# A short convolution before a maxout layer: the first GpSimd block later, ten such blocks for twelve, and a new early order

## The chip, the cores and the metric

The kernel runs on one core of a Trainium2 chip. The time is the device time of one execution in microseconds (us). Five runs of the kernel before gave a median of 463.79 us, from 463.38 to 464.07.

A core has TensorE (PE: matmuls, with weight loads listed apart as PEld), VectorE (DVE), ScalarE (ACT), GpSimd (POOL) and SyncE (SP, which here only issues DMAs). Each runs its own instructions in the order of the program and waits for the others by semaphores.

## The reference

x has 8 sequences of 4160 rows of 192 channels. First each channel is convolved along its sequence with seven taps: the taps of a head (24 channels share one) are the softmax of a row of `weight`, and rows ahead of the sequence are zero. The result, taken as 33280 rows y, goes through a maxout layer with 768 hidden values and back to 192 channels:

```python
out = np.einsum('hk,bskhg->bshg', softmax(weight), x_unf)   # x_unf: seven rows, shifted
h = np.maximum(np.maximum(y @ w1, y @ w2), y @ w3)
return h @ w_out
```

The kernel uses max(a, b, c) = max(a - c, b - c, 0) + c: `wd` holds w1 - w3 and w2 - w3, so that one Relu and one maximum give h - y w3, and the product y (w3 w_out), whose 192 x 192 matrix `m16` is made once, is added in the second layer.

## The kernel before

**Blocks.** The rows are cut into 65 blocks of 512 (`NB`), done one after the other by the loop over `t` at the end; blocks 0 and 1 are done ahead of it, together with the preparation of the weights. The convolution of a block is done in one of three ways.

- Blocks 0 to 3 (`conv_dense`, `cross`) use banded matmuls on fp16 copies of x, which give y with channels on partitions directly.
- Most blocks are *row blocks*. `load_x` (line 123) brings x as 70 rows (six of them for the overlap) times eight pieces; `cast_x` (L165, GpSimd, two instructions) makes it fp16; `conv` (L387) does a pair of blocks in 16 matmuls with a band matrix that has 70 rows and two column halves, a *burst*; `evac` (L438, two copies on ScalarE and two on VectorE) writes it to `ys`; `turn` (L447) transposes it by a DMA, so that channels come to partitions; and `double` (L457) copies the two halves of the partitions crosswise by two DMAs, so that both halves of the array have their operand. The tiles are named `yd`.
- Some are *GpSimd blocks*, whose indices are in `qpos` (L71): 11, 16, ... 61 and 64, twelve in all. `load_q` brings x (tile `xl`), `cast_q` makes it fp16, `turn_q` transposes it by a DMA (`xt<-xq`), `lead_q` copies the six rows ahead of it (`xt<-xt`), and `tap_q` (L221) does one tap at a time on GpSimd: three multiplications by a tap's weights (L229), one addition (L237, and L240 for the last). Then `double` follows as for the others.

**The layers.** `l1(t, j)` (L490) does a sixth of the hidden values: six matmuls of 64 rows and 512 columns. Two work at a time, one on the upper 64 rows of the array into `lp`, one on the lower 64 into `lq`; ScalarE takes the Relu of `lp` into `r` (L503), and VectorE the maximum of `r` and `lq` into `h` (L504). `lp` has two PSUM buffers (pool `psp`) and `lq` two (`psq`), and a burst takes one of each and two of `psw`. `st2(t, u, 6)` (L508) does a sixth of the second layer of the block before: matmuls of 64 rows and 192 columns, again on the upper and the lower half in turn (`i` = 0 and 1), five of each; ScalarE and VectorE add the halves (L560, L561) into `outs`, which `store` writes.

**One block of the loop** (L659 on). SP and GpSimd get their work first: the load of block t + 6, the crosswise copies for t + 2, the transposes and casts that are due, then the row block t + 5 is cast. Then comes `l1(t, 0)`, and, in two blocks of five, a burst (`convs_at`), three blocks ahead of the first of its pair. Just before the burst one matmul of the second layer is put, on the upper rows alone (`st2` with `first_half_only`, L536, a *filler*). Behind the burst come the evacuations, `turn(t + 3)`, the store of block t - 2, and the taps that `plan` gives to this block; then `st2(t - 1, 0)` and, in turn, the rest of both layers.

**The early blocks** have their own order. `plan` (L645 to L657) gives the first GpSimd block, 11, seven taps in blocks 5 to 8, and the last, 64, half a block for each tap; all between have their seven taps spread over five blocks, the first tap seven blocks ahead of the block itself. In block 2 SP loads blocks 7 and 8 and the first `xl`; in block 3 it issues the copies for block 4, the second `xl`, the transposes of blocks 5 and 6, the load of block 9, and `spread_w(0)` (L321, the seven weights of each channel written to DRAM as `wide`); in block 4 the copies for blocks 5 and 6. The store of block 0 is issued by GpSimd (L639), which has a queue of its own. In the preparation `make_wd(2, 4)` (L610) stands on VectorE behind `l1(0, 1)`.

Of the kernel before, what the change touches and what calls it, by code (L numbers as in the profile page):

```python
# [10 lines left out]
FP16 = mybir.dt.float16  # L11
# [3 lines left out]
P = 128  # L15
KW = 7
# [11 lines left out]
def kernel(  # L28
# [39 lines left out]
        blocks.append(segs)  # L68
    NB = len(blocks)
    EVERY = 5  # L70
    qpos = [q for q in range(11, NB - 3, EVERY)] + [NB - 1]  # L71
    qset = set(qpos)
    ENDS = NB - 7
    ends = blocks.pop()
# [33 lines left out]
    accp = ctx.enter_context(tc.tile_pool(name="accp", bufs=2))  # L108
    x16p = ctx.enter_context(tc.tile_pool(name="x16p", bufs=3))
    ysp = ctx.enter_context(tc.tile_pool(name="ysp", bufs=3))  # L110
    ydp = ctx.enter_context(tc.tile_pool(name="ydp", bufs=6))
    rp = ctx.enter_context(tc.tile_pool(name="rp", bufs=4))
    hp = ctx.enter_context(tc.tile_pool(name="hp", bufs=2))
    tp = ctx.enter_context(tc.tile_pool(name="tp", bufs=2))
# [332 lines left out]
    def turn(t):  # L447


        if t >= NB or t in qset:  # L450
            return
        t0, u, nu = place(t)
        yd = dense[t] = ydp.tile([P, 2, NCH // 2, P], FP16, tag="yd", name=f"yd_{t}")
        nc.sync.dma_start_transpose(out=yd[:, 0, :, :],
                                    in_=slots[t0][:, u, :, :].rearrange("p r d -> p (r d)"))

# [51 lines left out]
    def st2(t, u, NU, first_half_only=False):  # L508
# [24 lines left out]
        todo, ps = halves[t]  # L533
        n = len(todo[0])
        es = range(n * u // NU, n * (u + 1) // NU)
        for e in es[:1] if first_half_only else es:  # L536
            for i in range(2):
                if first_half_only:
                    if i:
                        break  # L540
                    ahead.add((t, e))
                elif i == 0 and (t, e) in ahead:
                    continue
                s, first, last, (a, b) = todo[i][e]
                b0 = s if t == NB - 1 else s - s % 2
                if (b0, i) not in ps:
                    pool, tag = (psw, "w")
                    if t == NB - 1 and s in (1, 2):
                        pool, tag = (psp, "p") if i == 0 else (psq, "q")
                    ps[b0, i] = pool.tile([P, 2, D], FP32, tag=tag, name=f"po{i}_{t}_{s}")  # L550
                nc.tensor.matmul(ps[b0, i][:, s % 2, :], lhsT=a, rhs=b, start=first, stop=last)  # L551
            ends = {todo[i][e][0] for i in range(2) if todo[i][e][2]}
            for s in sorted(ends):
                done[t, s] = done.get((t, s), 0) + sum(todo[i][e][0] == s and todo[i][e][2] for i in range(2))
                if done[t, s] < 2 or (s % 2 == 0 and t < NB - 1):
                    continue
                s0 = s if t == NB - 1 else s - 1
                ss = slice(s0 % 2, s % 2 + 1)
                a = tp.tile([P, 2, D], FP32, tag="a", name=f"a_{t}_{s}")
                nc.scalar.copy(out=a[:, ss, :], in_=ps[s0, 0][:, ss, :])  # L560
                nc.vector.tensor_add(out=outs[t][:, s0:s + 1, :], in0=a[:, ss, :],  # L561
                                     in1=ps[s0, 1][:, ss, :])
                if t == NB - 1 and s == 1:
                    store(t, 0, 2, (nc.sync,))
                elif t == NB - 1 and s == 3:
                    store(t, 2, 3, (nc.scalar,))
                    store(t, 3, 4, (nc.sync,))
# [37 lines left out]
    cast_w3(0)  # L605
    conv_dense(1, (nc.scalar.copy, nc.scalar.copy, nc.scalar.copy))
    cross(1)
    l1(0, 1)
    keep_warm(2)
    make_wd(2, 4)  # L610
    l1(1, 0)
    cast_w3(1)
    l1(1, 1, WW)
# [22 lines left out]
    l1(1, 5)  # L636
    for u in range(1, NJ):
        st2(0, u, NJ)
    store(0, 0, 4, (nc.gpsimd,))  # L639

# [2 lines left out]
    doubles_at = {2: (), 3: (4,), 4: (5, 6)}  # L645
    plan = {}
    for n, q in enumerate(qpos):
        w = min(4 + EVERY * n, NB - 7)
        load, cast, turned, lead = (1, 3, 4, 4) if n == 0 else (w - 6, w - 3, w - 2, w - 1)
        when = {0: (5, 5, 6, 6, 7, 7, 8), len(qpos) - 1: [w + k // 2 for k in range(KW)]}.get(  # L650
            n, [w + k * EVERY // KW for k in range(KW)])
        for what, at in (("load", load), ("cast", cast), ("turn", turned), ("lead", lead)):
            plan.setdefault(at, {})[what] = q
        for k in range(KW):
            plan.setdefault(when[k], {}).setdefault("taps", []).append((q, k))
    for t in range(2, NB):
        todo = plan.get(t, {})  # L657
        if t > 4:
            load_x(t + 6)  # L659
        for u in doubles_at.get(t, (t + 2,)):  # L660
            double(u)
        if t == 4:
            load_x(t + 6)
        if t > 3 and "turn" in todo:
            turn_q(todo["turn"])
        if t > 4 and "lead" in todo:
            lead_q(todo["lead"])
        if t > 3:
            cast_x(t + 5)
# [20 lines left out]
        if t == 2:  # L690
            turn(4)
            load_x(8)
            load_q(plan[1]["load"])
            cast_x(5)
            cast_x(6)
        elif t == 3:
            turn(5)
            turn(6)
            load_x(9)
            cast_x(7)  # L700
            cast_x(8)
        else:
            turn(t + 3)
        if t == 3:
            spread_w(0)
        if t == 4:
            spread_w(1)
            lead_q(todo["lead"])
        if 2 < t:
            store(t - 2, 0, 4, (nc.sync,))  # L710
        if "cast" in todo:
            cast_q(todo["cast"])
        for q, k in todo.get("taps", ()):
# [41 lines left out]
```

## Time and profile before

| | |
|---|---|
| five runs, median | 463.79 us |
| profiled execution: its time, its span | 463.79 us, 462.0 us |
| granted clock of TensorE | full speed in all 40 slices |
| share of the 16 DMA engines taken by SP's queue (q1) | 80.4% of the span |
| read from HBM, written to HBM | 29.85 MB, 25.56 MB |
| GpSimd: taps (L229), additions (L237, L240), casts of x (L176) | 116.1, 108.6, 21.7, 77.9 us |
| GpSimd waiting for x ahead of its casts | 59.0 us |
| VectorE: maximum (L504); ScalarE: Relu (L503) | 264.5 us; 230.5 us |

The span is what the profiler sees between the first and the last instruction; the time has 1.8 us around it. Busy times say how long an engine worked, not what the end waits for. The view that tells is the chain of work that ended last, followed back from the last instruction: each piece is there because the next one waited for it. The list of waits gives, for an engine and a line, whose work ended its idle time, with the total in us, how often, and the longest. A timeline gives start, length, engine, line and tiles of each instruction. For a DMA that SP issues, the length is that of the issue alone; the landing is a separate event in the trace (a semaphore that counts sixteen pieces).

### The profile page before, as it was taken

What the parts mean: (1) busy time and instruction counts of PE and PEld (TensorE: products, weight loads), DVE (VectorE), ACT (ScalarE), POOL (GpSimd) and SP (SyncE); (2) the same over time, 40 slices, a digit from 0 to 9 for tenths busy, and PEclk for the clock granted to TensorE, in tenths of its full rate; (3) what the DMA queues carried; (4) which work ended last, traced back from release to release, by engine and by line L of the source; (5) the groups of instructions that cost most, each with busy time, mean ns of one, the idle gap of its engine ahead of it and who ended that gap; (6) DMA issues with size and microseconds to landing.
All of it is one profiled execution on the core that took longest, in us unless ns stands there. A gap on an engine that the chain in (4) does not pass through costs nothing.

```text
span 462.0 us, 17259 instructions
## 1 busy us (share of the span) xinstructions
PE 454.4 (98%) x6969; PEld 369.2 (80%) x6969; DVE 354.2 (77%) x595; ACT 314.3 (68%) x597; POOL 352.5 (76%) x501
## 2 busy tenths in 40 slices
PE   8999899999999999999999999999999999999997
PEld 4577688977877887888888888888888888888886
DVE  6877677778787777777878777777878777777775
ACT  5767576667676666767676676766767676676664
POOL 5753399999977988978977968967968969969500
PEclk9999999999999999999999999999999999999999
DMA  8969999899878988788688697698598797874423
GB/s 189 222 147 211 168 188 184 197 206 225 187 127 200 191 164 214 176 179 188 164 184 189 159 217 174 148 208 201 134 210 177 167 222 176 159 176 92 100 70 104
DMA packets 137527, 80.77 MB, mean 175 GB/s; under 512 B 58294, under 2 KB 137368, under 8 KB 137448
## 3 DMA queue, kind: packets, MB, share of 16 engines
q1 hardware_dynamic: 137176, 79.18, 80.4%
q8 instruction: 54, 0.88, 0.9%
q0 software_dynamic: 112, 0.39, 0.3%
q14 instruction: 25, 0.20, 0.1%
q10 hardware_dynamic: 160, 0.10, 0.1%
HBM read 29.85 MB, written 25.56 MB: 120 GB/s over the span
## 4 chain that ended last, share of the span: by engine, by line
PE 90%; POOL 5%; DMA 3%; issue 1%; DVE 0%; ACT 0%; SPq 0%; POOLq 0%; DVEq 0%
PE lq L499 35%; PE po L551 33%; PE lp L499 14%; PE G L397 4%; POOL tap L237 2%; POOL tap L229 2%; DMA xf<-in_x_dram 2%; PE idle L294 1%; DMA xt<-xq 1%; PE D L415 1%; DMA xt<-xt 1%; POOL x L176 1%; PE lw L499 0%; PE band_cols L335 0%; DVE wd L352 0%
## 5 line engine op out<-in xcount | busy, mean ns | idle before, releaser
L504 DVE TENSOR_TENSOR h<-r,lq 128x512 f16<-128x512 f16 x386 | 264.5, 685 | 99.4 <-ACT r L503 99.1
L503 ACT ACTIVATE r<-lp 128x512 f16<-128x512 f32 x386 | 230.5, 597 | 134.5 <-PE lp L499 123.6
L499 PE MATMUL lp<-yd,wd 64*128 64x512 f16 x1158 | 312.3, 376 | 1.9 <-DMA yd<-yd 1.4
L499 PE MATMUL lq<-yd,wd 64*128 64x512 f16 x1158 | 312.1, 376 | 0.4 <-DVE yd L431 0.4
L551 PE MATMUL po<-wo,h 64*128 64x192 f16 x3120 | 263.2, 243 | 0.0
L551 PEld LDWEIGHTS <-h 64*128 64x128 f16 x3120 | 209.0, 94 | 21.1 <-issue 0.3
L499 PEld LDWEIGHTS <-wd 64*128 64x128 f16 x2340 | 161.9, 94 | 38.6 <-DMA yd<-yd 2.0
L176 POOL CAST x<-xf 70x768 f16<-70x768 f32 x98 | 77.9, 823 | 59.1 <-DMA xf<-in_x_dram 59.0
L229 POOL TENSOR_SCALAR tap<-xt,wcol 128x256 f32<-128x256 f16 x252 | 116.1, 478 | 5.7 <-DMA xt<-xt 5.3
L237 POOL TENSOR_TENSOR tap<-tap,tap 128x768 f32<-128x768 f32 x60 | 108.6, 1810 | 5.0
L551 PE MATMUL po<-m,yd 64*128 64x192 f16 x780 | 109.0, 243 | 0.0
L561 DVE TENSOR_TENSOR o<-a,po 128x384 f32<-128x384 f32 (+1 forms) x132 | 71.4, 541 | 0.6 <-ACT a L560 0.6
L551 PEld LDWEIGHTS <-yd 64*128 64x128 f16 x780 | 61.7, 94 | 11.7
L560 ACT COPY a<-po 128x384 f32<-128x384 f32 (+1 forms) x132 | 62.2, 472 | 2.3 <-PE po L551 2.3
L443 DVE CAST ys<-G 128x384 f16<-128x384 f32 x49 | 24.9, 549 | 0.7 <-PE G L397 0.6
L397 PEld LDWEIGHTS <-band 70*64 70x64 f16 x400 | 15.8, 110 | 10.0 <-PE lp L499 9.1
L240 POOL TENSOR_TENSOR yd<-tap,tap 128x768 f16<-128x768 f32 x12 | 21.7, 1812 | 1.0
L397 PE MATMUL G<-x,band 70*64 70x192 f16 (+1 forms) x400 | 21.2, 248 | 0.8 <-POOL x L176 0.8
L443 ACT CAST ys<-G 128x384 f16<-128x384 f32 x49 | 21.1, 483 | 0.9 <-DMA yd<-yd 0.9
L198 POOL CAST xq<-xl 128x384 f16<-128x384 f32 x24 | 11.4, 505 | 0.0
L256 POOL CAST xz<-xf 112x80 f16<-112x80 f32 (+2 forms) x18 | 5.2, 330 | 4.5 <-DMA xf<-in_x_dram 3.5
L294 PE MATMUL idle<-idle 128*128 128x512 f16 x15 | 6.6, 590 | 1.2 <-DVE idle L289 1.2
(52 smaller groups left out, 68.5 us busy)
## 6 DMA issues: line engine op xcount, KB each, us to landing
out_dram<-o SPq DMA_DIRECT2D x61, 384.0 KB
xf<-in_x_dram SPq DMA_DIRECT2D x47, 420.0 KB
yd<-yd SPq DMA_DIRECT2D x122, 96.0 KB
xl<-in_x_dram SPq DMA_DIRECT2D x12, 384.0 KB
xf<-in_x_dram SPq DMA_DIRECT2D x5, 367.5 KB
ws<-in_moe_w_dram SPq DMA_DIRECT2D x6, 192.0 KB
out_dram<-o SPq DMA_DIRECT2D x5, 192.0 KB
yd<-ys SPq DMA_TRANSPOSE x49
```

The costliest lines, as they stand in the source:

```text
L176: nc.gpsimd.tensor_copy(out=x16s[t0][0:K, :, c, u, :, :].rearrange("p h r c -> p r h c"), in_=xf[0:K, c:NR:2, :].rearrange("p r (h c) -> p ...
L229: nc.gpsimd.tensor_scalar(out=part[:, 2 * c:2 * c + 2, :], in0=xt[:, 2 * c:2 * c + 2, LEAD - PAD + k:LEAD - PAD + k + P], scalar1=wcol[:, ...
L237: nc.gpsimd.tensor_add(out=accs[q][:], in0=accs[q][:], in1=part[:])
L240: nc.gpsimd.tensor_add(out=yd[:, 0, :, :], in0=accs.pop(q)[:], in1=part[:])
L397: nc.tensor.matmul(G[h // per][HALF * c:HALF * (c + 1), h % per, :], lhsT=band[0:HALF + PAD, h, PAD:HALF + PAD], rhs=x16s[t0][0:HALF + PAD ...
L443: copy(out=slots[t][:, :, :, GRP * per * i:GRP * per * (i + 1)].rearrange("p u r (h c) -> p h (u r) c", c=GRP), in_=G[i][:].rearrange("p h ...
L499: nc.tensor.matmul(ps[i][:, 0:N], lhsT=wd[row, c, P * j:P * (j + 1)], rhs=y_all(t, i, c), start=(c == 0), stop=(c == NC - 1))
L503: nc.scalar.activation(out=r[:, 0:N], in_=ps[0][:, 0:N], func=AF.Relu)
L504: nc.vector.tensor_max(out=hs[t][:, j, 0:N], in0=r[:, 0:N], in1=ps[1][:, 0:N])
L551: nc.tensor.matmul(ps[b0, i][:, s % 2, :], lhsT=a, rhs=b, start=first, stop=last)
L560: nc.scalar.copy(out=a[:, ss, :], in_=ps[s0, 0][:, ss, :])
L561: nc.vector.tensor_add(out=outs[t][:, s0:s + 1, :], in0=a[:, ss, :], in1=ps[s0, 1][:, ss, :])
```

## The change

- GpSimd blocks are 15, 20, ... 60: ten for twelve. All have their taps by the same rule; the special cases for the first and the last are gone. So block 15's first tap is due in block 8, and blocks 11, 16, 61, 64 and so on become row blocks or change places. The row blocks are 51 in place of 49: one more pair, one more burst.
- Row blocks are loaded seven blocks ahead in place of six, and on SP the load stands behind the crosswise copies. In block 2 SP loads block 9 in place of the first `xl`, in block 3 block 10 in place of the second `xl` and block 9; the first `xl` comes in block 4.
- `spread_w(0)` and `spread_w(1)` move from blocks 3 and 4 to blocks 4 and 5, behind the copies that are issued at the head of these blocks.
- The store of block 0 goes from GpSimd's queue to SP's, in block 2, behind the loads.
- `make_wd(2, 4)` goes ahead of `l1(0, 1)` on VectorE.
- Two fillers stand ahead of each burst.
- The tiles `yd` of row blocks get a pool of their own with six buffers; the others keep four.

```diff
--- before.py
+++ after.py
@@ -68,7 +68,7 @@
         blocks.append(segs)
     NB = len(blocks)
     EVERY = 5
-    qpos = [q for q in range(11, NB - 3, EVERY)] + [NB - 1]
+    qpos = [q for q in range(15, NB - 4, EVERY)]
     qset = set(qpos)
     ENDS = NB - 7
     ends = blocks.pop()
@@ -108,7 +108,8 @@
     accp = ctx.enter_context(tc.tile_pool(name="accp", bufs=2))
     x16p = ctx.enter_context(tc.tile_pool(name="x16p", bufs=3))
     ysp = ctx.enter_context(tc.tile_pool(name="ysp", bufs=3))
-    ydp = ctx.enter_context(tc.tile_pool(name="ydp", bufs=6))
+    ydp = ctx.enter_context(tc.tile_pool(name="ydp", bufs=4))
+    ypp = ctx.enter_context(tc.tile_pool(name="ypp", bufs=6))
     rp = ctx.enter_context(tc.tile_pool(name="rp", bufs=4))
     hp = ctx.enter_context(tc.tile_pool(name="hp", bufs=2))
     tp = ctx.enter_context(tc.tile_pool(name="tp", bufs=2))
@@ -450,7 +451,7 @@
         if t >= NB or t in qset:
             return
         t0, u, nu = place(t)
-        yd = dense[t] = ydp.tile([P, 2, NCH // 2, P], FP16, tag="yd", name=f"yd_{t}")
+        yd = dense[t] = ypp.tile([P, 2, NCH // 2, P], FP16, tag="yp", name=f"yp_{t}")
         nc.sync.dma_start_transpose(out=yd[:, 0, :, :],
                                     in_=slots[t0][:, u, :, :].rearrange("p r d -> p (r d)"))
 
@@ -533,7 +534,7 @@
         todo, ps = halves[t]
         n = len(todo[0])
         es = range(n * u // NU, n * (u + 1) // NU)
-        for e in es[:1] if first_half_only else es:
+        for e in es[:2] if first_half_only else es:
             for i in range(2):
                 if first_half_only:
                     if i:
@@ -605,9 +606,9 @@
     cast_w3(0)
     conv_dense(1, (nc.scalar.copy, nc.scalar.copy, nc.scalar.copy))
     cross(1)
+    make_wd(2, 4)
     l1(0, 1)
     keep_warm(2)
-    make_wd(2, 4)
     l1(1, 0)
     cast_w3(1)
     l1(1, 1, WW)
@@ -636,7 +637,6 @@
     l1(1, 5)
     for u in range(1, NJ):
         st2(0, u, NJ)
-    store(0, 0, 4, (nc.gpsimd,))
 
 
 
@@ -645,25 +645,24 @@
     doubles_at = {2: (), 3: (4,), 4: (5, 6)}
     plan = {}
     for n, q in enumerate(qpos):
-        w = min(4 + EVERY * n, NB - 7)
-        load, cast, turned, lead = (1, 3, 4, 4) if n == 0 else (w - 6, w - 3, w - 2, w - 1)
-        when = {0: (5, 5, 6, 6, 7, 7, 8), len(qpos) - 1: [w + k // 2 for k in range(KW)]}.get(
-            n, [w + k * EVERY // KW for k in range(KW)])
+        w = q - 7
+        load, cast, turned, lead = max(4, w - 6), w - 3, w - 2, w - 1
         for what, at in (("load", load), ("cast", cast), ("turn", turned), ("lead", lead)):
-            plan.setdefault(at, {})[what] = q
+            assert what not in plan.setdefault(at, {})
+            plan[at][what] = q
         for k in range(KW):
-            plan.setdefault(when[k], {}).setdefault("taps", []).append((q, k))
+            at = w + k * EVERY // KW
+            assert at < q - 2
+            plan.setdefault(at, {}).setdefault("taps", []).append((q, k))
     for t in range(2, NB):
         todo = plan.get(t, {})
-        if t > 4:
-            load_x(t + 6)
         for u in doubles_at.get(t, (t + 2,)):
             double(u)
-        if t == 4:
-            load_x(t + 6)
-        if t > 3 and "turn" in todo:
+        if t > 3:
+            load_x(t + 7)
+        if "turn" in todo:
             turn_q(todo["turn"])
-        if t > 4 and "lead" in todo:
+        if "lead" in todo:
             lead_q(todo["lead"])
         if t > 3:
             cast_x(t + 5)
@@ -690,24 +689,22 @@
         if t == 2:
             turn(4)
             load_x(8)
-            load_q(plan[1]["load"])
+            load_x(9)
             cast_x(5)
             cast_x(6)
         elif t == 3:
             turn(5)
             turn(6)
-            load_x(9)
+            load_x(10)
             cast_x(7)
             cast_x(8)
         else:
             turn(t + 3)
-        if t == 3:
+        if t == 4:
             spread_w(0)
-        if t == 4:
+        if t == 5:
             spread_w(1)
-            lead_q(todo["lead"])
-        if 2 < t:
-            store(t - 2, 0, 4, (nc.sync,))
+        store(t - 2, 0, 4, (nc.sync,))
         if "cast" in todo:
             cast_q(todo["cast"])
         for q, k in todo.get("taps", ()):
```

## The prediction

> **What bounds the kernel now.** I read the page's busy times first, then the waits of TensorE, then the chain that ended last, then the timelines of SP and TensorE around the places that the chain names. From the page, parts 1 and 4:
>
> ```profile
> PE 454.4 (98%) x6969; PEld 369.2 (80%) x6969; DVE 354.2 (77%) x595; ACT 314.3 (68%) x597; POOL 352.5 (76%) x501
> ...
> PE 90%; POOL 5%; DMA 3%; issue 1%; DVE 0%; ACT 0%; SPq 0%; POOLq 0%; DVEq 0%
> ```
>
> TensorE is the bound, but 8% of the chain is GpSimd and DMA. The waits of TensorE (total, times, longest) name the two places:
>
> ```profile
> PE lp L499 <- DMA yd<-yd: 1.4, 1, 1.4
> ...
> PE G L397 <- POOL x L176: 0.8, 2, 0.5
> ```
>
> The chain in order of time (start, length, piece) shows where they lie, and what the steady state costs:
>
> ```profile
> 42.92 7.04 DMA xf<-in_x_dram
> 50.02 5.07 DMA xt<-xq
> 55.15 3.14 DMA xt<-xt
> ...
> 78.59 1.54 POOL x L176 x2
> 80.18 0.82 PE G L397 x15
> ...
> 215.17 0.85 PE G L397 x16
> ...
> 228.85 0.85 PE G L397 x16
> ...
> 248.93 0.85 PE G L397 x16
> ```
>
> After 100 us nothing but TensorE stands on the chain. From the starts of the first-layer groups in the TensorE timeline (1.06 apart, six to a block) a block takes 6.36. Two blocks with one convolution burst take 228.85 - 215.17 = 13.68, three with one 20.08; so a burst costs 0.96 or 1.00, **0.98 on average**.
>
> Block starts in the same timeline give the early losses. Blocks 3, 4, 5 begin at 35.02, 42.53, 51.67 and block 6 at 58.13: 23.11 us, where two blocks with a burst and one without need 2 x 7.34 + 6.36 = 21.04. **2.07 lost.** Block 9 takes 8.35 instead of 7.36: **0.99 lost.** Nothing else from block 3 on is over its price.
>
> **Part 1, ten GpSimd blocks for twelve.** Two blocks go from GpSimd to TensorE, which is one more pair, one more burst (24 to 25 of the paired kind): **+0.98**. Its four evacuations (2 x 483 ns on ScalarE, 2 x 549 ns on VectorE) lie in that price, for the bursts that I measured have them too. GpSimd loses 2 x (21 x 0.478 + 6 x 1.81 + 2 x 0.505 + 0.2) = 44 us and gains four casts, 4 x 0.823 = 3.3 us. It is off the path after 100 us, so that is worth nothing there.
>
> **Part 2, the first GpSimd block at 15.** The taps of block 11 were due from block 5 (51.67) but began at 58.47, after late transfers, and are squeezed into 3.5 blocks; so the casts of blocks 12 and 13 stood behind them until 80.13, and block 9's burst waited. Now the first tap is due at block 8, spread over five blocks like all later ones, which never wait. GpSimd casts block 9 in block 4 and block 10 in block 5, ahead of their burst in block 6. **-0.99**; bounds -0.99 and 0.
>
> **Part 3, the early order on SP.** Block 4 needs the two copies that complete its operand (issued at 38.00), block 5 the next two (44.95). From SP's timeline (start, length of issue):
>
> ```profile
> 34.92 0.44 SPq L188 DMA_DIRECT2D xl<-in_x_dram  x1
> 38.00 1.14 SPq L462 DMA_DIRECT2D yd<-yd  x2
> 39.18 0.59 SPq L188 DMA_DIRECT2D xl<-in_x_dram  x1
> 39.88 2.94 SPq L454 DMA_TRANSPOSE yd<-ys  x2
> 42.92 0.52 SPq L144 DMA_DIRECT2D xf<-in_x_dram  x1
> 43.49 0.84 SPq L324 DMA_DIRECT2D wide<-line  x1
> 44.38 0.47 SPq L580 DMA_DIRECT2D out_dram<-o  x1
> 44.95 3.82 SPq L462 DMA_DIRECT2D yd<-yd  x4
> ```
>
> The trace's landing events show a queue that is served in this order: the `xl` of 34.92 lands at 41.40, the copies at 42.48 and 42.79 (block 4 starts at 42.53), the transposes at 44.35 and 44.99, the `xf` at 49.96, `wide` at 50.16, the store at 51.40, and block 5's first copy at 51.62 (block 5 starts at 51.67).
>
> *Block 5's copies.* Of the `xf` of 42.92 most pieces are in by 47.4; then DMA thins out (205 GB/s in 47-49 us, 148 in 49-51, after 250 in 45-47) and the store behind it lands 3 us later, though a store elsewhere follows its forerunner by 1.15 (214.97 to 216.13). Between them stands only `wide`, 192 pieces of 14 bytes written to DRAM. I take it as the cause. The Trainium skill (DMA: Bandwidth & Descriptors, Specifications) says that transfers under 512 B are done as read-modify-write; that would fit, and this trace shows the delay but not its mechanism. The change moves `wide` a block later, behind these copies. Then they land at 45.0 (transposes) + 2.4 (`xf`) + 1.15 (store) + 0.25 = 48.8, before block 5 can start. If `wide` is innocent they land near 51.6 as now.
>
> *Block 4's copies.* Ahead of them the queue had `xl` (512 pieces of 768 B). Now it has block 9's `xf` (560) and block 0's store (512), which leaves GpSimd's queue for SP's. Reads ran at 283 pieces per us (566 in 38-40), stores at 450 (900 in 214-216): + 48/283 + 512/450 = +1.3. Off that goes about 0.2, since the store no longer runs beside the first transfers (it landed at 32.77): landing near 42.48 + 1.1 = 43.6. Without a wait block 4 would start at 35.02 + 7.34 = 42.36. So it waits 1.3, +0.1 for the second copy (0.12 now). Bounds: most of the 16 pieces of the first copy are in by 41.1 now, one is late at 42.48; without the late one the wait is 0, and with another `xf` like the 7.04 one (5 us where 2.4 is usual) it is 3.9.
>
> So block 5 starts at 42.36 + 1.4 + 7.34 = 51.1, its copies there already: of 2.07 lost, 1.4 stays. **-0.67**; bounds -2.07 and +1.8. The stall does not go; it moves a block forward.
>
> The Trainium skill (the same page, Issuing engines are not separate DMA queues) says that DMAs of all engines share the same engines, and another queue saves only issue time. By that, moving the store costs nothing and this term would be -1.8. Here the row differs, for order counts: issued at 28.61 the store was through before the copies joined; on SP's queue it stands ahead of them.
>
> **Part 4, loads seven ahead, more buffers, loads behind the copies on SP.** SP waits up to 3.4 us (42.3 in all) at such copies for a transpose, and each load behind is now that much later, but a whole block (6.36) earlier in the program. GpSimd's waits for `xf` (59 us) go; they held nothing except in part 2. Separate pools keep SP's transposes from waiting for a buffer; TensorE doesn't wait for them after 100 us. 0.
>
> **Part 5, early VectorE order.** `make_wd(2, 4)` (0.95) goes ahead of the maximum of l1(0, 1), from 15.32 to about 14.72. TensorE's wait for it (0.57 at 16.33) would go, but l1(0, 2) also takes the PSUM buffer that this maximum frees, and that now ends at 14.72 + 0.95 + 0.69 = 16.36. The one wait takes the other's place: 0; bounds -0.57 and +0.95.
>
> **Part 6, two fillers.** A filler is a second-layer matmul on the upper 64 rows, put ahead of the burst, while the lower rows still stream:
>
> ```profile
> 214.67 0.38 PE L499 MATMUL lp<-yd,wd 64*128 64x512 f16 x1
> 214.87 0.38 PE L499 MATMUL lq<-yd,wd 64*128 64x512 f16 x1
> 214.89 0.24 PE L551 MATMUL po<-m,yd 64*128 64x192 f16 x1
> 215.17 0.85 PE L397 MATMUL G<-x,band 70*64 70x192 f16 x16
> 215.96 0.26 PE L551 MATMUL po<-m,yd 64*128 64x192 f16 x2
> ```
>
> In all 24 bursts the first band weights load 303 to 305 ns after the last `lq` starts, however long the filler has run (180 to 300 ns). So the lower rows set the burst. A second filler starts 82 ns after the first (the pitch of such matmuls), where 160 to 220 ns are free. And behind the burst the lower rows still have their five matmuls before the next `lp`, which never overtakes them. I take 0. Bounds: 82 ns off each of 25 bursts, -2.05; or 82 ns on each, +2.05.
>
> **Sum**, against the profiled execution (463.79 for a span of 462.0; the median of the five is 463.79 too): 0.98 - 0.99 - 0.67 + 0 = -0.68, so **463.1 us**. Runs within 0.2% (462.86 to 464.72) can't be told from no change here.
>
> **Rivals.**
> 1. *The early waits go altogether*: block 4's copies land in time, for the one late piece is chance. For it: 15 of its 16 pieces are in by 41.58 now. Against: the store is in the way. 0.98 - 0.99 - 2.07 = -2.08: 461.7.
> 2. *Fillers pay*: 82 ns off each burst. For it: the upper rows idle there. Against: the fixed 304 ns. 463.1 - 2.05 = 461.05.
> 3. *Slower: the second filler holds the band's weights back*, as it may if they wait for its end (243 ns) rather than its stream: at 82 ns a burst 465.15. It decides from (464.72 - 463.1)/25 = 65 ns a burst. Against: a filler 180 ns old didn't hold them.
> 4. *GpSimd is not relieved*: another burst waits as block 9's did, 464.1. Against: five blocks per seven taps never waited.
>
> **Chances.** Forecast 0.52 (462.3 to 463.9; 0.17 of it faster, 0.35 the same); rival 1 0.18; rival 2 0.08; rival 3 0.10; rival 4 0.08 (same); a new early wait of over 1.6 us 0.04. Faster 0.17 + 0.18 + 0.08 = 0.43; same 0.35 + 0.08 = 0.43; slower 0.14. The range takes in rival 1 and the small end of rival 3: 461.2 to 464.7.
>
> **What would show it.** Block 4 starting near 43.6 and block 5 near 51.1 (part 3; block 5 still near 51.7 with its copies late would clear `wide`); block 9 without GpSimd ahead of its burst; 25 bursts whose weights load 304 ns after `lq`; 6.36 per block. A burst price off 0.98, or waits of TensorE after block 6, would make it wrong.

## The result, and the profile after

The kernel after took 467.48 us (median of 53 runs, 463.18 to 475.47); the kernel before, beside it, 464.26 (95 runs, 462.59 to 469.66). The ratio is **1.0045 [1.0032, 1.0059]**: slower by about 2.1 us, where 0.7 less was forecast. Single runs of this kernel scatter far more than those before, and the ratio leaves out those over 1.5% above the fastest (13 of 53), so it is smaller than the quotient of the medians (1.0069). The forecast of 463.1 is where its quickest runs lie.

The profiled execution took 470.98 us, 3.5 more than the median, with a span of 469.1. The page's busy times and shares of the chain:

```profile
PE 455.6 (97%) x6985; PEld 357.1 (76%) x6985; DVE 354.9 (76%) x597; ACT 317.6 (68%) x599; POOL 311.2 (66%) x444
...
PE 91%; DMA 6%; DVE 1%; SPq 1%; issue 0%; POOL 0%; ACT 0%; DVEq 0%; POOLq 0%
```

GpSimd has left the chain (5% before) and has 41 us less to do, as meant. DMA has doubled its share to 6%. The list of waits, over all engines (total, times, longest):

```profile
DVE o L562 <- DMA out_dram<-o: 3.6, 2, 3.1
PE lq L500 <- DVE h L505: 3.5, 3, 2.9
...
PE lp L500 <- DMA yp<-yp: 2.2, 1, 2.2
```

The third line is the early wait for the crosswise copies, as before. The first two are new: VectorE's addition of the halves, into an output buffer, waits for a *store* out of that buffer, and TensorE then for VectorE. (Lines are one higher than before: L500 is the first layer, L505 the maximum, L562 the addition, L581 the store.) The chain in order of time shows both places:

```profile
32.93 5.76 DMA yp<-ys
38.76 6.90 DMA yp<-yp
...
114.42 0.60 ACT r L504
115.04 0.42 DVE h L505
115.46 6.42 DMA out_dram<-o
122.48 0.69 DVE h L505
...
214.10 0.81 PE G L398 x16
227.77 0.81 PE G L398 x16
```

The store issued at 115.46 lands at 121.88, and TensorE's work stands behind it. Two blocks with one burst take 227.77 - 214.10 = 13.67 at the end of the list, as they did (13.68).

The starts of the blocks (first matmul of `l1(t, 0)` in the TensorE timeline) cut the span into stretches. A second profile of the same kernel, and two of the experiments below, stand beside:

| us | before | after | after, again | loads first | loads first, more PE |
|---|---|---|---|---|---|
| to block 2 | 27.05 | 27.87 | 28.15 | 27.11 | 27.33 |
| block 2 to block 6 | 31.08 | 31.52 | 30.77 | 30.91 | 29.53 |
| block 6 to block 64 | 391.45 | 396.08 | 396.59 | 390.89 | 390.89 |
| block 64 to the last matmul | 9.15 | 9.19 | 9.19 | 9.19 | 9.19 |
| last matmul to the end | 3.28 | 4.43 | 4.10 | 4.33 | 3.40 |
| span | 462.01 | 469.10 | 468.80 | 462.43 | 460.34 |

The differences of after add up to 0.83 + 0.44 + 4.63 + 0.04 + 1.15 = 7.09. Nearly all is in the long stretch, and there in three blocks: 13 (+0.53 over its price), 14 (9.84, +3.48) and 15 (8.50, +1.19), 5.2 in all. In the second profile it is blocks 20 and 23 to 25 (+5.7): the place changes from one execution to the next. **The end is the other: 0.8 to 1.2 us more between the last matmul and the end, in both.**

Not all of the 5.2 is waiting. TensorE stands still for 0.35 us at 113.42 and for 2.90 us at 120.31, 3.25 in all. Just behind that pause its granted clock is half of full speed for 3.41 us, from 123.64 to 127.05. The first line here is the granted clock in 40 slices of the span, in tenths (9 is 90% or more); the others are bursts from the chain, of which the second falls into that stretch:

```profile
PEclk8999999999899999999999999999999999999999
...
107.76 0.81 PE G L398 x16
...
126.28 1.20 PE G L398 x16
...
146.67 0.78 PE G L398 x16
```

Block 15 waits for nothing; its 1.19 us lie in that stretch. Half of 3.41 is 1.7 us, my estimate of the cost: with the waits 4.95 of the 5.2. The second profile has the same, a pause of 2.44 us at 188.22 and half the clock from 190.60 to 194.01. The kernel before and loads first have no such stretch before their last matmul.

### The profile page after: what moved, and what is told of

Read it like the earlier page. It is cut to its first block, busy times and chain, and to the rows that moved or that the text cites. A ratio compares the mean times of both kernels' runs of the same rounds, so it can differ in the third digit from the quotient of the medians.

```text
span 469.1 us, 17240 instructions
## 1 busy us (share of the span) xinstructions
PE 455.6 (97%) x6985; PEld 357.1 (76%) x6985; DVE 354.9 (76%) x597; ACT 317.6 (68%) x599; POOL 311.2 (66%) x444
## 4 chain that ended last, share of the span: by engine, by line
PE 91%; DMA 6%; DVE 1%; SPq 1%; issue 0%; POOL 0%; ACT 0%; DVEq 0%; POOLq 0%
PE lq L500 39%; PE po L552 36%; PE lp L500 11%; PE G L398 4%; DMA xf<-in_x_dram 2%; DMA yp<-yp 1%; DMA out_dram<-o 1%; DMA yp<-ys 1%; PE D L416 1%; PE lw L500 1%; DVE h L505 1%; SPq L270 0%; POOL xz L257 0%; SPq L145 0%; PE pm L381 0%
## 5 line engine op out<-in xcount | busy, mean ns | idle before, releaser
L505 DVE TENSOR_TENSOR h<-r,lq 128x512 f16<-128x512 f16 x386 | 264.3, 685 | 99.8 <-ACT r L504 97.1
L552 PE MATMUL po<-wo,h 64*128 64x192 f16 x3120 | 273.7, 243 | 0.0
L500 PE MATMUL lq<-yp,wd 64*128 64x512 f16 x918 | 247.4, 376 | 3.3 <-DVE h L505 3.3
L500 PE MATMUL lp<-yp,wd 64*128 64x512 f16 x918 | 248.2, 377 | 2.2 <-DMA yp<-yp 2.2
L500 PEld LDWEIGHTS <-wd 64*128 64x128 f16 x2340 | 158.1, 94 | 50.7 <-issue 5.6
L230 POOL TENSOR_SCALAR tap<-xt,wcol 128x256 f32<-128x256 f16 x210 | 96.7, 477 | 55.9 <-DMA xt<-xt 55.9
L177 POOL CAST x<-xf 70x768 f16<-70x768 f32 x102 | 81.1, 822 | 29.5 <-DMA xf<-in_x_dram 22.4
L238 POOL TENSOR_TENSOR tap<-tap,tap 128x768 f32<-128x768 f32 x50 | 90.4, 1809 | 4.2
L552 PE MATMUL po<-m,yp 64*128 64x192 f16 x612 | 92.6, 244 | 0.0
L562 DVE TENSOR_TENSOR o<-a,po 128x384 f32<-128x384 f32 (+1 forms) x132 | 71.4, 541 | 4.5 <-DMA out_dram<-o 3.6
L500 PE MATMUL lp<-yd,wd 64*128 64x512 f16 x240 | 66.0, 381 | 0.5 <-DVE wd L353 0.5
L500 PE MATMUL lq<-yd,wd 64*128 64x512 f16 x240 | 65.6, 380 | 0.2 <-DVE h L505 0.2
L552 PEld LDWEIGHTS <-yp 64*128 64x128 f16 x612 | 50.7, 94 | 14.0 <-issue 0.3
L552 PE MATMUL po<-m,yd 64*128 64x192 f16 x168 | 23.8, 243 | 0.0
```

Source lines behind the costliest of these rows:

```text
L177: nc.gpsimd.tensor_copy(out=x16s[t0][0:K, :, c, u, :, :].rearrange("p h r c -> p r h c"), in_=xf[0:K, c:NR:2, :].rearrange("p r (h c) -> p ...
L230: nc.gpsimd.tensor_scalar(out=part[:, 2 * c:2 * c + 2, :], in0=xt[:, 2 * c:2 * c + 2, LEAD - PAD + k:LEAD - PAD + k + P], scalar1=wcol[:, ...
L238: nc.gpsimd.tensor_add(out=accs[q][:], in0=accs[q][:], in1=part[:])
L500: nc.tensor.matmul(ps[i][:, 0:N], lhsT=wd[row, c, P * j:P * (j + 1)], rhs=y_all(t, i, c), start=(c == 0), stop=(c == NC - 1))
L505: nc.vector.tensor_max(out=hs[t][:, j, 0:N], in0=r[:, 0:N], in1=ps[1][:, 0:N])
```

## Where the late wait comes from: the order on SP

Why is a store late at 115? SP's timeline of after (start, length of issue):

```profile
102.89 1.13 SPq L463 DMA_DIRECT2D yp<-yp  x2
104.12 0.53 SPq L145 DMA_DIRECT2D xf<-in_x_dram  x1
104.75 1.23 SPq L204 DMA_TRANSPOSE xt<-xq  x1
106.08 1.47 SPq L455 DMA_TRANSPOSE yp<-ys  x1
107.63 0.54 SPq L581 DMA_DIRECT2D out_dram<-o  x1
111.62 1.11 SPq L463 DMA_DIRECT2D yp<-yp  x2
```

The copies of 102.89 had to wait for their transpose; only then comes the load (its last piece lands at 108.73), and the transposes are queued behind it: that of 106.08 lands at 111.61. At 111.62 SP goes on, for the next copies wait for just that transpose. So copies, load and transpose form one chain, one turn of it 8.73 us here, where a block takes 6.36 or 7.32, and the stores of each block stand behind it on SP. In the kernel before, the load goes out ahead of the copies and runs while SP waits for them. The two sides in the lists of SP's waits, after:

```profile
SPq L463 <- DMA yp<-ys: 106.9, 50, 3.7
```

and the kernel after with its loads ahead of the copies again (e1_load_first):

```profile
SPq L463 <- DMA yp<-ys: 54.4, 41, 3.7
```

Before it was 42.3. The longest wait hardly differs; the sum does. From 90 to 420 us a transpose from `ys` lands (median) 3.06 us after its issue before, 4.52 in after and 3.78 with the loads first. I call *lag* the time from the start of a block to the issue of its store (that of block t - 2). Before, it is 1.6 to 5.6 us from block 12 on. In after it is 8.2 in block 4 and 13.0 in blocks 7 and 8, then 10.3, 11.9, 13.6 in blocks 9 to 11 and 15.0 in block 12. That is the store of block 10, and with its 6.42 to the landing its buffer is free 21.4 us after block 12 began. There are three output buffers, so the addition of block 13 needs it again, and VectorE was ready for that 18.5 us after block 12 began (118.91): it waits 3.1.

My theory at this point: it is the order alone, with the long stretch of row blocks (5 to 14) that the later first GpSimd block leaves. Rivals: the store of block 0 on SP (part 3), or the fillers (part 6).

**After, unchanged** (e1_after_again, beside the next three on one chip).

> The changed kernel itself, a second profile of it. Theory A (SP's loop: the load of x stands behind the crosswise copies, which wait for a transpose, so stores come late and VectorE waits for an output buffer): about 1.0045 times the kernel before, and the profile again has waits of VectorE for the landing of a store somewhere in blocks 12 to 16, of 1 to 5 us in all, besides 1.3 to 2.5 us lost in block 3. Rival B (only the early order costs): time 1.0045 as well, but nothing lost after block 5; the 5.2 us lost in blocks 13 to 15 of the first profile would be an accident of that execution.

469.08 (464.71 to 471.33), 1.0094 [1.0061, 1.0128].

**Loads first** (e1_load_first):

```diff
+        if t > 4:
+            load_x(t + 7)
         for u in doubles_at.get(t, (t + 2,)):
             double(u)
-        if t > 3:
+        if t == 4:
             load_x(t + 7)
```

> The changed kernel with the load of x back ahead of the crosswise copies on SP from block 5 on, still seven blocks ahead. Theory A: no wait in blocks 12 to 16, 2 to 4 us less than the changed kernel of the same call, so 0.995 to 1.000 of the kernel before; the loss in block 3 stays. Rival B: same time as the changed kernel, within 0.5 us. Rival C (too much DMA work in the stretch of row blocks from 5 to 14, whatever the order): waits in blocks 12 to 16 stay, gain under 1 us.

464.40 (463.50 to 466.17), 1.0002 [0.9983, 1.0022]. The scatter is gone, no wait for a store is in the profile, and the lag is at most 5.4 us from block 12 on. This one edit is worth 4.7 us between the medians: without the new order the late wait does not come. The granted clock is part of it: the clock lost, (1 - granted share) x span, averages 1.9 us over the ten runs of after and 0.4 over these twelve, so by this estimate about 1.5 of the 4.3 us between their means is clock.

**The store of block 0 on GpSimd's queue again** (e1_store0_pool):

```diff
-        store(t - 2, 0, 4, (nc.sync,))
+        store(t - 2, 0, 4, (nc.sync if t > 2 else nc.gpsimd,))
```

> The changed kernel with the store of block 0 back on GpSimd's queue, still in block 2. Theory A: the loss ahead of block 4 falls by the store's 1.1 to 1.5 us, the waits in blocks 12 to 16 stay; 0 to 1.5 us less than the changed kernel. Rival B: 2 us or more less than the changed kernel, no loss after block 5.

469.42 (464.36 to 473.50), 1.0090 [1.0060, 1.0121]: as slow as after, so this rival is out. That rests on the times: the profile is of one of the quicker runs (465.99), its lag is at most 11.0 from block 12 on, and no late wait is in it.

**One filler** (e1_one_filler):

```diff
-        for e in es[:2] if first_half_only else es:
+        for e in es[:1] if first_half_only else es:
```

> The changed kernel with one filler ahead of each burst as before. In the first profile of the changed kernel a burst cost 0.957 us each time, in the kernel before 0.96 and 1.00 in turn. If the second filler is what takes the 0.04 off every second burst, bursts cost 0.96 and 1.00 again and the time is 0.5 us longer than the changed kernel; if it does nothing, bursts stay at 0.957 and the time is the same within 0.3 us.

468.68 (464.25 to 475.51), 1.0056 [1.0024, 1.0088]: slow too, and VectorE waits 4.0 us for stores in its profile, so the second filler is not the cause either.

**The order in the kernel before** (e2_before_load_behind), and **a fourth output buffer in after** (e2_outs4):

```diff
-        if t > 4:
-            load_x(t + 6)
         for u in doubles_at.get(t, (t + 2,)):
             double(u)
-        if t == 4:
+        if t > 3:
             load_x(t + 6)
```

> The kernel before with one part of the change alone: from block 5 on the load of x stands behind the crosswise copies on SP (six blocks ahead as before). Theory A: SP's waits at the copies for a transpose rise from 42 us to 80 or more, stores come late, and it is 1 to 6 us slower than the kernel before, with a wide spread; waits of VectorE for a store's landing or of TensorE for casts appear after block 9. Rival C (the longer stretch of row blocks is what overloads the queue, the order matters only there): within 0.5 us of the kernel before.

```diff
-    outp = ctx.enter_context(tc.tile_pool(name="outp", bufs=3))
+    outp = ctx.enter_context(tc.tile_pool(name="outp", bufs=4))
```

> The changed kernel with four output buffers in place of three. If the late stores cost time through the output buffer alone, the waits of VectorE for a store's landing go, and the time falls by 2 us or more against the changed kernel (to about 1.000 to 1.004 of the kernel before); SP's waits at the copies stay near 115 us. If SP's lateness reaches TensorE by another way as well (copies or casts late), the time stays within 1 us of the changed kernel.

The first took 464.48 (463.19 to 465.83), **1.0007 [0.9984, 1.0030]**. SP waits 115.8 us at its copies, more than in after, and the lag hovers between about 5 and 10 us; but it never climbs to 15, and nothing that TensorE needs is late. So the order alone is not enough: what else of the change it takes (the long stretch, the loads seven blocks ahead or another part) this run does not say. The second took 464.66 (463.01 to 470.94), 1.0010 [0.9982, 1.0038]: SP waits as in after (101.2 us), the lag reaches 11.5, and 9 of 12 runs lie between 463.0 and 465.1. Of the 53 runs of after 10 are that quick. In most runs, then, the buffer is the way by which the late store reaches TensorE. But three runs took 469.0 to 470.9. What they wait for no profile shows; their granted clock was 0.991 to 0.994, that of the other nine 0.998 to 1.0.

**The long stretch taken away** (e4_after_q11): the first GpSimd block at 11 again, prepared in blocks 2 to 5, with ten such blocks (11 to 56) and all else as in after:

```diff
-    qpos = [q for q in range(15, NB - 4, EVERY)]
+    qpos = [q for q in range(11, NB - 8, EVERY)]
...
-        load, cast, turned, lead = max(4, w - 6), w - 3, w - 2, w - 1
+        load, cast, turned, lead = (2, 3, 4, 5) if n == 0 else (max(4, w - 6), w - 3, w - 2, w - 1)
...
-            at = w + k * EVERY // KW
+            at = (5, 5, 6, 6, 7, 7, 8)[k] if n == 0 else w + k * EVERY // KW
...
-        if t == 4:
+        if t == 3:
             spread_w(0)
-        if t == 5:
+        if t == 4:
             spread_w(1)
```

> The changed kernel, its load still behind the copies, with ten GpSimd blocks at 11, 16, ... 56 in place of 15 to 60 (the first with its taps in blocks 5 to 8 and the seven weights spread in blocks 3 and 4, as in the kernel before). If the ten row blocks in a row at the start are what drives SP late when its order is the changed one, SP's stores stay within 12 us of their place, no wait for a store's landing shows, and the time is 2 us or more below the changed kernel, 0.999 to 1.003 of the kernel before. If the order alone does it, it is as slow and as widely spread as the changed kernel (1.005 to 1.010).

471.90 (471.39 to 475.64), 1.0187 [1.0160, 1.0214]. No store is late in its profile (lag at most 10.6). But block 9 loses 5.2 us behind late taps (3.2 of it waiting for casts; the clock is at half for 3.41 us behind that), and in such a pause SP catches up: the lag falls from 10.4 to 2.6. So it does not tell whether the stretch or the pause keeps the lag down: that both the order *and* the stretch are needed is not shown. The second profile of after speaks against it in part: there the late store is waited for in block 24, where every fifth block is a GpSimd block as before, though the lag had stayed above 9 since block 5.

**Stores issued by ScalarE** (e3_stores_act). This was to take the stores out of SP's chain and leave the order as it is:

```diff
-        store(t - 2, 0, 4, (nc.sync,))
+        store(t - 2, 0, 4, (nc.scalar if 2 < t < NB - 4 else nc.sync,))
```

> The changed kernel, its load still behind the copies, with the stores of blocks 1 to 58 issued by ScalarE on its own queue, when their block's turn comes. If it is SP's order of issue alone that makes stores late, no wait of VectorE for a store's landing is left in the profile, and the time falls by 2 us or more against the changed kernel, to 0.998 to 1.002 of the kernel before, with a narrow spread; if the DMA engines themselves are behind, the stores land late on any queue and waits stay, as slow and as widely spread as the changed kernel.

550.29 (545.63 to 556.95), 1.1829 [1.1782, 1.1877], for another reason. The chain of this kernel in a window:

```profile
202.79 2.17 DMA yp<-yp
...
205.04 0.42 ACTq L581
```

ScalarE's issue comes right after the landing of copies (204.96) whose data it has no use for. In the trace both DMAs count on one semaphore, of which the kernel's DMAs share eight; 21 of the 60 DMAs that ScalarE issues behind an earlier one on the same semaphore start 0.07 to 0.08 us after its landing, and none before it. So ScalarE's Relus stand behind SP's waits: they wait 57.8 us for copies. About 28 of the 86 us over the kernel before lie in the clock, whose granted share averages 0.948 here (the estimate from above). The question that the run was meant for stays open.

## The early order, and `wide`

**Copies ahead** (e2_copies_first, on loads first): the copies for block 4 go ahead of block 9's load and block 0's store, which stood before them in SP's queue.

```diff
         for u in doubles_at.get(t, (t + 2,)):
             double(u)
+        if t == 3:
+            load_x(9)
+            store(0, 0, 4, (nc.sync,))
...
-            load_x(9)
...
-        store(t - 2, 0, 4, (nc.sync,))
+        if t > 2:
+            store(t - 2, 0, 4, (nc.sync,))
```

> The changed kernel with loads ahead of the copies, and in block 3 the copies for block 4 ahead of the load of block 9 and of the store of block 0, which follow them and so stand between these copies and the two transposes. If the loss in block 3 comes from what stands ahead of the copies on SP's queue and from the transposes directly behind them, block 3 takes 7.3 to 7.7 in place of 8.9, block 4 waits at most 0.5, and the time is 1.0 to 1.8 us less than with the loads ahead alone: 0.996 to 0.998 of the kernel before. If the loss is due to the lateness of the first transpose, it stays.

464.57 (462.15 to 467.25), 1.0008 [0.9986, 1.0030]. Block 4 now starts with no wait (42.84, block 3 + 7.31), where 1.55 were lost in loads first. Block 5 then waits 1.83, and the stretch from block 2 to 6 takes 30.90 against 30.91. In this pair the order says only which block pays; that the early transfers as a whole are the limit is my reading of it.

**Both, and the end mended** (e3_copies_first_more_pe: the same, with block 1's store behind the copies for 5 and 6, and the extra instructions of the next section):

```diff
         if t == 4:
+            store(1, 0, 4, (nc.sync,))
             load_x(t + 7)
...
-        if t > 2:
+        if t > 3:
             store(t - 2, 0, 4, (nc.sync,))
```

> Loads ahead of the copies, the early 76 TensorE instructions, the copies for block 4 ahead of the load of block 9 and the store of block 0, and the store of block 1 behind the copies for blocks 5 and 6. With the copies for block 4 first, block 5 waited 1.8 us for its own; with one store less ahead of them it should wait 0.5 to 1.0. Then blocks 3 to 5 lose 0.5 to 1.0 in all, and the time is 0.994 to 0.998 of the kernel before. If the transposes and not the queue set these landings, block 5 loses 1.8 again: 0.998 to 0.999.

464.12 (461.55 to 465.48), 0.9989 [0.9968, 1.0010]: blocks 4 and 5 wait 0.1 together, but block 2 takes 1.05 and block 6 0.5 over their price. No gain.

**Block 0's store on GpSimd's queue, block 10's load ahead of the transposes, more PE** (e3_store0_cushion_more_pe, on loads first):

```diff
         elif t == 3:
+            load_x(10)
             turn(5)
             turn(6)
-            load_x(10)
...
-        store(t - 2, 0, 4, (nc.sync,))
+        store(t - 2, 0, 4, (nc.sync if t > 2 else nc.gpsimd,))
```

> Loads ahead of the copies, the early 76 TensorE instructions, the store of block 0 on GpSimd's queue, and the load of block 10 between the copies for block 4 and the two transposes. In earlier profiles the second copy landed together with the start of the transposes that stood directly behind it, up to 1.4 us after the first. If the transposes hold it, the second copy lands 0.3 to 0.5 after the first here, block 3 loses under 0.5, block 5 up to 1, and the time is 0.995 to 0.998 of the kernel before. If not, block 3 loses 1.5 to 2.5 as with the store on GpSimd's queue alone.

465.14 (463.11 to 468.58), 1.0023 [0.9999, 1.0047]. Block 4's copies landed at 44.00 and 44.21, behind block 9's load (43.27): without the store they still come 0.7 us behind that load.

**`wide` a block later in the kernel before** (e4_before_wide_later), and the same with two fillers (e4_before_wide_fillers):

```diff
-        if t == 3:
-            spread_w(0)
         if t == 4:
+            spread_w(0)
+        if t == 5:
             spread_w(1)
+        if t == 4:
             lead_q(todo["lead"])
```

> The kernel before with one thing changed: the small writes of `wide`, and the reads of it, one block later, so that they are issued behind the copies for blocks 5 and 6. If the small writes hold up what stands behind them, block 5's copies land by 50.0 in place of 51.6, blocks 4 and 5 lose under 0.7 in place of 1.8, and the time is 1.0 to 1.7 us less: 0.9963 to 0.998. If `wide` is innocent, block 5's copies land at 51.6 as before and the time is the same.

> The same with two fillers ahead of each burst: bursts of 0.957 each in place of 0.957 and 1.00, so 0.5 us less than `wide` later alone: 0.995 to 0.997 of the kernel before if `wide` is the cause, 0.999 if it is innocent.

471.50 (470.62 to 474.09), 1.0167 [1.0144, 1.0190], and 470.27 (469.22 to 470.99), 1.0128 [1.0110, 1.0145]. In the first profile block 5's first copy still landed at 51.51 (51.62 before), its transposes at 46.09 (44.99). From the second transpose to that copy it took 6.63, 6.00 and 5.51 us in three profiles with `wide` between them, 5.42 and 4.74 in the two without. The means differ by 1 us, the nearest two by 0.1: of the 3 us that I had put on `wide` at most about 1 shows, and two profiles against three do not settle even that. And there is a wait that the kernel before does not have:

```profile
POOL wcol L331 <- DMA wcol<-wide: 7.7, 1, 7.7
```

The taps need these weights. They begin at 63.7 us in place of 58.5, the casts of the next row blocks come behind them, and block 9 loses 8.15 in place of 1.0 (9.39 in the other kernel). That is the mechanism of part 2, made larger by hand: late taps, late casts, a burst that waits. TensorE waits 6.05 and 5.93 us there; nearly all the rest is clock again, at half for 6.83 us in the first kernel and 10.24 in the second, a stretch that begins during that wait and ends at 89.11 and 91.30.

## The end: one packet of program

In the trace TensorE's program is fetched in packets of 16 KB (queue q8 on the page: 54 in the kernel before, 55 in after). Each takes about 1 us on one of the 16 DMA engines (median 1.16 before, 1.15 in after; 0.88 to 1.94). Before, the last one passes at 452.5 us. The kernel after has 16 matmuls more, and its last packet passes at 464.6, while the last stores go out; in loads first at 457.99, taking 1053 ns. There the last store lands 2.6 us after its issue (458.79 to 461.38), where it took 1.7 before (459.44 to 461.10).

Theory: this packet is the extra 1 us of the end. A rival: the end is longer for SP's load of late stores. If the packet is to blame, instructions added early move it away from the end. The added ones do the small matmuls that make the band's columns a second time. Against the rival: in loads first no store is late, and the end takes 4.33 all the same.

**Loads first, more PE** (e2_more_pe, on loads first):

```diff
-    for c in range(WIN):
+    for c in [*range(WIN), *range(WIN)]:
         nc.tensor.matmul(bps[:, c, :], lhsT=line[:, WIN - 1 - c:WIN + 31 - c],
```

> The changed kernel with loads ahead of the copies, and the 38 small matmuls that make the band computed twice at the start, while TensorE only idles: 76 more TensorE instructions. In all profiles of kernels with one pair more, a packet of 16 KB of program passes one DMA engine just as the last stores go out (457.99 in a span of 462.4) and the last store lands 1 us later than in the kernel before. If that is the cause, the packet comes 2 to 3 us earlier now, the time from the last matmul to the end of the span is 3.3 us in place of 4.3, and the time falls by 0.5 to 1.0 us. If not, the tail stays at 4.3.

462.94 (461.97 to 466.12), **0.9975 [0.9950, 1.0000]**. The last packet passes at 454.4, and the end takes 3.40 us (3.28 before, 4.33 in loads first). All three kernels with these instructions have an end of 3.4 to 3.5; of those with one pair more and without them the ends are 4.1 to 4.5, but 3.86 with four output buffers and 3.60 with the copies ahead. The packet's own end orders them all:

| the last packet ends | end of the span after the last matmul |
|---|---|
| over 1.5 us before the last matmul ends (five kernels with 54 packets, three with the added instructions) | 3.26 to 3.51 |
| 0.20 us after it (copies ahead) | 3.60 |
| 0.45 us after it (four output buffers) | 3.86 |
| 0.73 to 0.81 us after it (three profiles) | 4.07 to 4.22 |
| 0.85 to 1.10 us after it (four profiles) | 4.33 to 4.45 |

The later the packet ends, the longer the end, in profiles with a late wait and without: that is the packet's doing. This is the quickest kernel of the study, though its interval ends at 1.0: more work, placed so that a fetch falls elsewhere. Against loads first, which ran on another chip, the end gives 0.93 us; the rest of the difference in the profiles (1.38 from block 2 to 6) lies in a stretch that varies that much from one execution to the next.

## Fillers alone

**Two fillers in the kernel before** (e3_before_two_fillers):

```diff
-        for e in es[:1] if first_half_only else es:
+        for e in es[:2] if first_half_only else es:
```

> The kernel before with two fillers ahead of each burst and nothing else: that part of the change alone. In the changed kernel a burst costs 0.957 us each time, in the kernel before 0.957 and 1.00 in turn. If the second filler does that, all bursts cost 0.957 here and the time is 0.5 us less than the kernel before (ratio 0.9990); the prediction's working (nothing) has bursts of 0.96 and 1.00 and the same time; its rival, a weights load held back, has 2 us more.

463.50 (462.79 to 467.75), 0.9997 [0.9972, 1.0021]. The block starts tell more than the time. With one filler, blocks with a burst take 7.317 and 7.36 in turn (before and e1_one_filler); with two, always 7.317 (here and in after). That is 0.04 us off every second burst, 0.5 in all. The band's weights still load 304 ns after the last `lq` starts. But the next `lp` comes 264 ns behind the first matmul after the burst, in place of 343: the lower rows do not hold it back as far as I had taken it.

## Why the prediction was wrong, step by step

The stretches of the table, with other profiles beside them, show each term. Without a late wait they come to this: from block 6 to 64, 390.89 - 391.45 = -0.56; from block 2 to 6, about -0.6 (below); end +1.05. Together about zero, and loads first measured 1.0002. After adds the late wait.

- **Part 4, the loads behind the copies: predicted 0, measured about 4.7 us** (469.08 to 464.40 on one chip; 5.2 in the profile, 3.25 of it waits of TensorE and about 1.7 the half clock behind them). This is the step that failed: "each load behind is now that much later, but a whole block (6.36) earlier in the program. ... 0." I followed the load that was moved, and not what stands behind it on SP's queue: the transposes that the next copies wait for, and the stores, whose buffers are needed again within 18.5 us.
- **Part 1, one more burst: right, and not whole.** Predicted +0.98, measured 0.957. Its evacuations lie in it. But its 16 matmuls also moved the last fetch of program to the end, +1.05, which no term held.
- **Part 2: right.** Block 9 takes 6.36 and the burst behind it waits for no cast. Predicted -0.99, measured -1.03 (0.04 of it the second filler's); the `wide` runs show the same mechanism.
- **Part 3: direction right, one reason wrong.** The stall moved from block 5 to block 4: block 5 starts 7.33 behind block 4, its copies in at 51.11 and 51.49 while it starts at 53.03. I said block 4 near 43.6; it started at 45.70, of which 0.8 came from block 2's start and 1.1 from block 0's store, which landed 2.22 us behind block 9's load (43.08 to 45.30) where I had 1.14; in loads first it took 1.12. From block 2 to 6, six profiles with the new order take 29.5 to 31.5, mean 30.34, three with the old 30.9 to 31.1, mean 30.97: -0.6, where -0.67 was forecast; as one execution can be off by 1, the agreement may be luck. Of what I put on `wide` about a third shows at most. The Trainium skill (DMA: Bandwidth & Descriptors, Issuing engines are not separate DMA queues) would have the store's move cost nothing; the one profile that differs from after in this alone took 33.21 from block 2 to 6 with the store on GpSimd's queue, against 31.52 and 30.77 without; 3.41 us at half the clock lie in that stretch (from 46.12), about 1.7 by the estimate above. So taking it off SP brought no gain there; whether it cost something, one execution can't say.
- **Part 5: not settled, one reading wrong.** Block 2 started at 27.87. I said that the wait for `wd` would go and one for `h` take its place; in after TensorE still waits 0.53 us for `wd` (which now takes 1.51 us on VectorE in place of 0.95) and then 0.20 for `h`. Over five profiles with the old order block 2's start is 26.4 to 27.6, over twelve with the new 26.5 to 28.1, means 26.9 and 27.2; in the profiled execution the second load of x lands at 4.97 against 4.32, and the granted clock is at half from 7.58 to 10.99.
- **Part 6: predicted 0, measured -0.5 us in the profiles.** "Never overtakes them" was wrong: the next `lp` starts 80 ns sooner. It is less than the time alone can tell.

Of the rivals none came. The third ended on the right side with the wrong mechanism, and the weights' 304 ns speaks against it. What I had named as a sign, "waits of TensorE after block 6", is what came. No term, and no rival, held a change of the clock.

Open: why three runs with four output buffers took 469 us or more, what the order needs beside it to do harm (the long stretch, or the loads seven blocks ahead, which no run takes back alone), and why the late wait comes in some executions only, and at different blocks.

## What to carry to other kernels

Where a queue issues in order and some of its DMAs wait, price a move by what stands behind it: write out one turn of the queue (wait, issue, landing, next wait) and compare it with the time of a block. A store that is off the chain has a deadline too, its buffers times the block. And a time that is unchanged says little of a queue: in the kernel before with its load behind the copies SP waited 115.8 us there in place of 42.3, at the same time. The lag of the stores showed the state of the queue long before anything waited.

## What was new of the hardware

- Fetching the program takes DMA time: 55 packets of 16 KB here, about 1 us each on one engine. With one that ends 0.2 to 1.1 us behind the last matmul the end takes 3.60 to 4.45 us, with the last one gone before it 3.26 to 3.51.
- A pause of TensorE can cost more than its length: behind the pauses of 2.90 and 2.44 us in the two profiles of after the granted clock was at half for 3.41 us. A pause of 2.2 us ahead of block 4 in after was not followed by one.
- In these kernels an issue waits until the earlier DMA on its semaphore has landed, across engines: with stores from ScalarE, which waited for SP's copies, the kernel took 550.29 us where the kernel before took 464.31.
- The same transposes land later by what stands ahead of them in the queue (medians): 3.06 us after their issue in the kernel before and 4.84 with its load behind the copies; 4.52 in after and 3.78 with the loads first.
